# Token-major attention outputs, x turned by DMA, and v cast in GpSimd-queue DMAs

## The chip, the cores and the metric

One Trainium2 chip, one of its cores. The metric is the device time of one execution in microseconds. Each kernel ran several times; medians are given with the number of runs. A ratio is the mean time of one kernel's fast runs over that of the other's fast runs of the same rounds, with a 95% interval, so it is not quite the ratio of the two medians. Runs that the chip made in its slower state (a lower granted clock and a time some per cent longer) are left out of every ratio; the medians are over all runs, slow ones included. Profiles show one execution; its span is some 1.5 to 2 us shorter than the time.

## The reference

Two stages in a row. A gated linear attention over 4 batches of 8 heads, 768 tokens each, head size 48:

```
state[t] = sigmoid(f_logit[t]) * state[t-1] + outer(k[t], v[t])
y[t]     = q[t] @ state[t]                      # per batch and head
```

Then, with x the 3072 tokens by 384 columns that the heads' outputs make side by side:

```
h = x @ w_in                  # 384 -> 2048
out = (h * cos(h)) @ w_out    # 2048 -> 384, float32
```

Inputs and output are float32. `q`, `k`, `v` and `f_logit` lie in DRAM as (batch, head, token, 48), so what one token and one head have in a row is 48 numbers, 192 bytes.

## The kernel before

The tokens are cut into 24 chunks of 128. A chunk loads f, v, k and q (192 KB each), makes decayed q and k in bf16 (`qk`), transposes them (`qkt`: by TensorE for the first six chunks, by DMA later), multiplies them to masked scores (`am`), updates the state (`sz`), and makes the attention output. A list scheduler in the kernel's own Python (class `Plan`) places all operations before anything is emitted: it gives each a cost and a delay, and its order becomes the fixed order of instructions on each engine.

The attention output is made with features on partitions, directly as `xT`, the form that the second stage needs. Heads of 48 do not fit blocks of 128, so v and the state lie in zero-padded tiles and windows of 128 columns are cut out of them: 16 matmuls of 128 columns for a chunk with a state, from two kinds:

```python
VW = D + 128
vzS = slots("vz", 4, [128, H * VW + 128], zero=700.0)    # zero-padded v, bf16
...
P.op({"POOL": 510.0}, lambda e: nc.gpsimd.tensor_copy(   # cast of v, one per chunk
    out=vz.ap[:, 128:].rearrange(...)[:, :, 0:D], in_=vf.ap), reads=[vf], writes=[vz], prio=prio)
...
if kind == "a":                                           # 10 of these
    nc.tensor.matmul(o[:, t, :], lhsT=vz.ap[:, w0:w0 + 128],
                     rhs=ams[n // 4].ap[:, n % 4, :], **fl)
else:                                                     # 6 of these
    nc.tensor.matmul(o[:, t, :], lhsT=S_in.ap[:, n, w0:w0 + 128],
                     rhs=qdt.ap[:, n, :], **fl)
```

The loads (192-byte pieces):

```python
ap = src[b, :, c * C:(c + 1) * C, :].rearrange("h p d -> p h d")
...
P.op({"SP": 1080.0}, lambda e, t=t, ap=ap: nc.sync.dma_start(out=t.ap, in_=ap),
     writes=[t], prio=prio, lat=2200.0)
...
P.op({"SP": 2000.0}, lambda e: nc.sync.dma_start_transpose(out=qkt.ap, in_=qk.ap), ...)
```

The eight weight loads go through the GpSimd queue with a cast, and cos is a sine with a bias read from a tile (`bias=halfpi`).

Of the kernel before, what the change touches and what calls it, by code (L numbers as in the profile page):

```python
# [91 lines left out]
class Op:  # L92
    __slots__ = ("seq", "eng", "fn", "prio", "table", "deps", "vals", "alloc", "start",
                 "end", "lat", "waiting", "after", "grp", "frees")


class Plan:


    SEM = 70.0  # L100

# [3 lines left out]
    def op(self, eng, fn, reads=(), writes=(), prio=0.0, table=None, lat=0.0, grp=None):  # L105
        o = Op()
        o.seq, o.fn, o.prio, o.table, o.lat, o.grp = len(self.ops), fn, prio, table, lat, grp
        o.eng, o.frees = eng, None
        o.deps, o.alloc, o.vals = set(), [], []
        for v in reads:  # L110
            o.deps.update(v.writers)
        for v in writes:
            w = getattr(v, "whole", v)
            if w.pool is not None:
                o.alloc.append(w)
            if v.writers:

                o.deps.add(v.writers[-1])
        for v in list(reads) + list(writes):
            v = getattr(v, "whole", v)  # L120
            if v.pool is not None and v not in o.vals:
                o.vals.append(v)
                v.uses += 1
        for v in writes:
            v.writers.append(o)
        o.after = []
        self.ops.append(o)
        return o
# [6 lines left out]
    def run(self):  # L135
        engs = ("PE", "ACT", "DVE", "POOL", "SP")
        free = dict.fromkeys(engs, 0.0)
        table, lock = "E", None
        left = {}
# [9 lines left out]
        while len(order) < n:  # L149
            best = None  # L150
            for o in ready:
                at = max([d.end + (0.0 if e0 == d.eng == "PE" else self.SEM)
                          for d in o.deps for e0 in (next(iter(o.eng)),)], default=0.0)
                ok = True
                for v in o.alloc:
                    if v.slot is not None:
                        continue
                    b = v.pool.best()
                    if b is None:
                        ok = False  # L160
                        break
                    at = max(at, b[0] + self.SEM)
                if not ok:
                    continue
                pick = None
                for e, cost in o.eng.items():
                    if e == "ACT" and lock is not None and o.grp != lock and o.table is not None:
                        continue
                    s = max(at, free[e])
                    sw = 1300.0 if e == "ACT" and o.table not in (None, table) else 0.0  # L170
                    if pick is None or s + cost + sw < pick[0]:
                        pick = (s + cost + sw, s, e, cost)
                if pick is None:
                    continue
                key = (pick[1], o.prio, o.seq)
                if best is None or key < best[0]:
                    best = (key, pick[1], o, pick[2], pick[3])
# [16 lines left out]
            o.start, o.end = s, s + cost + o.lat  # L194
            free[e] = s + cost
            o.eng = e
# [20 lines left out]
def kernel(  # L217
# [10 lines left out]
    nc = tc.nc  # L228
# [12 lines left out]
    NPE = 6  # L241
# [31 lines left out]
    vS = slots("v", nld, [128, H, D], F32)  # L273
# [4 lines left out]
    VW = D + 128  # L278
    vzS = slots("vz", 4, [128, H * VW + 128], zero=700.0)
    qktS = slots("qkt", 4, [128, 3 * NP, C])  # L280
    amS = slots("am", 4, [128, 4, C])
    SW = 128 + 2 * D + 128
    szS = slots("sz", 3, [128, NP, SW], zero=650.0)
# [26 lines left out]
    def load_weights(part, i, prio):  # L310
        if part == 0:
            dst = w_in_v[i]
            src = moe_w_in.rearrange("(km p) f -> p km f", p=128)[:, :, i * 512:(i + 1) * 512]
        else:
            dst = w_out_v[i]
            src = moe_w_out.rearrange("(kf p) m -> p kf m", p=128)[:, i * 4:(i + 1) * 4, :]
        o = P.op({"SP": 2000.0}, lambda e, dst=dst, src=src: nc.gpsimd.dma_start(
            out=dst.ap, in_=src), writes=[dst], prio=prio, lat=2500.0)
        o.deps.add(first_v[0])
# [5 lines left out]
    first_v = []  # L325

    def chunk_load(b, c, prio):
        vals = []
        for pool, src in ((fS, f_logit), (vS, v), (kS, k), (qS, q)):
            t = Val(pool)  # L330
            ap = src[b, :, c * C:(c + 1) * C, :].rearrange("h p d -> p h d")
            if prio < 1 and pool in (kS, qS):
                P.op({"ACT": 600.0}, lambda e, t=t, ap=ap: nc.scalar.dma_start(out=t.ap, in_=ap),
                     writes=[t], prio=prio, lat=3300.0)
            elif prio < 2 and pool in (vS, qS):
                o = P.op({"POOL": 1000.0}, lambda e, t=t, ap=ap: nc.gpsimd.dma_start(out=t.ap, in_=ap),
                         writes=[t], prio=prio, lat=3300.0)
            else:
                P.op({"SP": 1080.0}, lambda e, t=t, ap=ap: nc.sync.dma_start(out=t.ap, in_=ap),  # L339
                     writes=[t], prio=prio, lat=2200.0)  # L340
            vals.append(t)
        return vals
# [42 lines left out]
    def attend(b, c, ld, bt, bi, prio):  # L385
# [3 lines left out]
        qk, vz = Val(qkS), Val(vzS)  # L389
# [9 lines left out]
        for par in range(2):  # L399
            P.op({"POOL": 550.0, "DVE": 350.0} if fast else {"POOL": 550.0}, lambda e, par=par: E(e).tensor_mul(  # L400
                out=ktd[par].ap, in0=kf.ap[:, par:H:2, :],
                in1=bi.ap.rearrange("p (h d) -> p h d", d=D)[:, par:H:2, :]),
                reads=[kf, bi], writes=[ktd[par]], prio=prio)
        o = P.op({"POOL": 510.0}, lambda e: nc.gpsimd.tensor_copy(  # L404
            out=vz.ap[:, 128:].rearrange("p (h w) -> p h w", w=VW)[:, :, 0:D], in_=vf.ap),
            reads=[vf], writes=[vz], prio=prio)
        first_v.append(o)
# [27 lines left out]
        else:  # L435
            P.op({"SP": 2000.0}, lambda e: nc.sync.dma_start_transpose(out=qkt.ap, in_=qk.ap),
                 reads=[qtd] + ktd, writes=[qdt] + kz, prio=prio, lat=2500.0)
# [22 lines left out]
        if c < NCH - 1:  # L460
            ps, S_out = Val(miS), Val(szS)

            def pes(e):
                o = ps.ap[:, 0:H * D].rearrange("p (h d) -> p h d", d=D)
                for h in range(H):
                    nc.tensor.matmul(o[:, h, :], lhsT=qk.ap[:, (NP + h) * C:(NP + h + 1) * C],  # L466
                                     rhs=vz.ap[:, 128 + h * VW:128 + h * VW + D],
                                     start=(h == 0), stop=(h == H - 1))
            P.op({"PE": 8 * 30.0}, pes, reads=ktd + [vz], writes=[ps], prio=prio, lat=170.0)
# [3 lines left out]
            else:  # L473
                st = Val(stS)
                P.op({"DVE": 530.0}, lambda e: nc.vector.tensor_add(  # L475
                    out=st.ap, in0=psv(), in1=S_in.ap[:, :, 128:128 + 2 * D]),
# [3 lines left out]
                out=S_out.ap[:, :, 128:128 + 2 * D], in0=srcap(),  # L480
# [5 lines left out]
        py = Val(miS)  # L486
        jobs = []
        for t in range(KM):
            for h in range(H):
                r = h * D - t * 128  # L490
                if -D < r < 128:
                    jobs.append((t, "a", h, r))
            if S_in is not None:
                for p in range(NP):
                    r = p * 2 * D - t * 128
                    if -2 * D < r < 128:
                        jobs.append((t, "s", p, r))

        def pey(e):
            o = py.ap.rearrange("p (a n) -> p a n", n=C)  # L500
            for i, (t, kind, n, r) in enumerate(jobs):
                first = all(j[0] != t for j in jobs[:i])
                fl = dict(start=(i == 0), stop=(i == len(jobs) - 1))
                if kind == "a":
                    w0 = 128 + n * VW - r
                    nc.tensor.matmul(o[:, t, :], lhsT=vz.ap[:, w0:w0 + 128],  # L506
                                     rhs=ams[n // 4].ap[:, n % 4, :], **fl)
                else:
                    w0 = 128 - r
                    nc.tensor.matmul(o[:, t, :], lhsT=S_in.ap[:, n, w0:w0 + 128],  # L510
                                     rhs=qdt.ap[:, n, :], **fl)
        rd = [vz, qdt] + ams + ([S_in] if S_in is not None else [])
        P.op({"PE": len(jobs) * N128}, pey, reads=rd, writes=[py], prio=prio, lat=170.0)
        x = xT[tok // C]

        def yev(e):
            d = x.ap
            s = py.ap[:, 0:KM * C].rearrange("p (a n) -> p a n", n=C)
            if e == "ACT":
                nc.scalar.copy(out=d, in_=s)  # L520
            else:
                nc.vector.tensor_copy(out=d, in_=s)
        P.op({"ACT": 380.0, "DVE": 530.0}, yev, reads=[py], writes=[x], prio=prio)


    def moe(t0, T):
# [6 lines left out]
        for j in range(KF // G):  # L533
            ph, co = Val(phS), Val(coS)

            def g1(e, j=j, ph=ph):
# [10 lines left out]
            P.op({"ACT": 640.0}, lambda e, ph=ph, co=co: nc.scalar.activation(  # L547
                out=co.ap, in_=ph.ap, func=AF.Sin, bias=halfpi),
# [6 lines left out]
        for i in range(T // 128):  # L555
# [12 lines left out]
            def ev(e, po=po, ot=ot):  # L568
# [7 lines left out]
                out=out[r0:r0 + 128, :], in_=ot.ap), reads=[ot], prio=pr, lat=2000.0)  # L576

    halfpi = cpool.tile([128, 1], F32, name="halfpi")
    nc.vector.memset(halfpi, HALF_PI)
# [59 lines left out]
```

## Time and profile before

| | before |
|---|---|
| time, median of 4 runs (lowest to highest) | 202.32 us (201.92 to 202.7) |
| span of the profiled run | 200.6 us |
| PE busy | 178.9 us |
| PE idle before 60 us / 60 to 160 us / after | 16.8 / 0.4 / 4.4 us |

The last row is worked out from windows: what PE was busy in a stretch, taken from the stretch's length. Two of them, with the columns as in the prediction below (stretch and length, PE, weight load, DVE, ACT, POOL, granted clock, DMA share, GB/s; the share is the packets' time added up, so it can pass 1):

```profile
20.00:30.00 10.00, 6.71 (x97) 5.97 (x95) 5.88 (x11) 5.60 (x9) 3.65 (x6) 0.88 1.27 211
60.00:160.00 100.00, 99.56 (x1081) 79.66 (x1079) 80.56 (x142) 87.22 (x151) 24.87 (x37) 1.00 1.01 205
```

```profile
PE ps L367 <- ACT sp L355: 6.3, 2, 5.3
PE ps L447 <- DMA qkt<-qk: 0.5, 1, 0.5
...
DVE am L452 <- PE ps L447: 3.2, 4, 1.9
```

From 60 to 160 us TensorE pauses 0.44 us in all, and in the whole execution it waits for a transposed `qkt` only once, for 0.5 us. L447 is the score product, L367 the first product of a chunk's decay. q1 is the queue of SP (SyncE), q0 that of GpSimd.

### The profile page before, as it was taken

The page shows a single profiled execution, that of the slowest core. Times are in us where ns is not written, and L with a number is a line of the kernel's source. Part 1 is how long each engine was busy: PE and PEld are TensorE (multiplying, and loading weights), DVE is VectorE, ACT ScalarE, POOL GpSimd, SP SyncE. Part 2 cuts the span into 40 slices and gives each one's busy share as a digit, 9 for nine tenths or more (in the row PEclk, how much of TensorE's full clock was granted, in tenths as well). Part 3 has the DMA queues.
Part 4 walks back from the last instruction along what each step waited for, and adds up shares of the span by engine and source line. Part 5 has one row for each costly group of instructions (what it writes and reads, how often), then busy time and mean ns, then how long its engine had stood idle before and what let it go on. Part 6 is the DMA issues. An engine that isn't in the chain of part 4 may idle for free.

```text
span 200.6 us, 5037 instructions
## 1 busy us (share of the span) xinstructions
PE 178.9 (89%) x1960; PEld 142.3 (71%) x1960; DVE 143.2 (71%) x248; ACT 151.6 (76%) x259; POOL 54.7 (27%) x86
## 2 busy tenths in 40 slices
PE   0359678989979999999999999999999999999992
PEld 0249566886859687778797887787787878678660
DVE  7865744775889979689689598597595998854500
ACT  4457745859999898798998799798796999727510
POOL 8775600230721130250201412711412315000000
PEclk9999978999999999999999999999999999999999
DMA  7999998998909999989999999899899954911012
GB/s 141 218 217 223 218 205 153 177 184 164 230 6 172 193 220 190 223 138 241 214 202 233 217 215 225 177 220 198 186 207 212 202 106 143 97 39 42 16 64 78
DMA packets 132328, 34.15 MB, mean 170 GB/s; under 512 B 125504, under 2 KB 132160, under 8 KB 132304
## 3 DMA queue, kind: packets, MB, share of 16 engines
q1 hardware_dynamic: 126320, 29.70, 73.8%
q0 software_dynamic: 3904, 3.74, 11.3%
q10 hardware_dynamic: 2080, 0.39, 1.1%
q8 instruction: 15, 0.25, 0.5%
q14 instruction: 9, 0.07, 0.1%
HBM read 25.17 MB, written 4.72 MB: 149 GB/s over the span
## 4 chain that ended last, share of the span: by engine, by line
PE 68%; DMA 13%; ACT 8%; issue 4%; POOL 2%; SPq 2%; DVE 2%; ACTq 0%; POOLq 0%
PE ps L561 28%; PE ps L540 26%; DMA qkt<-qk 5%; PE ps L447 5%; PE ps L506 4%; DMA w_in_bf<-in_moe_w_in_dram 4%; DMA v<-in_v_dram 4%; PE ps L510 2%; ACT b L377 2%; SPq L339 2%; PE ps L466 1%; ACT xT L520 1%; ACT qkt L430 1%; DVE qk L400 1%; ACT bi L377 1%
## 5 line engine op out<-in xcount | busy, mean ns | idle before, releaser
L540 PE MATMUL ps<-xT,w_in_bf 128*128 128x256 bf16 (+1 forms) x672 | 70.3, 259 | 4.8 <-DMA w_in_bf<-in_moe_w_in_dram 3.3
L551 DVE TENSOR_TENSOR gT<-ps,cosh 128x512 bf16<-128x512 f32 x96 | 60.7, 683 | 17.1 <-ACT cosh L547 17.0
L561 PE MATMUL ps<-w_out_bf,gT 128*128 128x384 bf16 x384 | 71.1, 329 | 0.0
L547 ACT ACTIVATE cosh<-ps,halfpi 128x512 bf16<-128x512 f32 x96 | 59.7, 694 | 10.1 <-PE ps L540 9.8
L540 PEld LDWEIGHTS <-w_in_bf 128*128 128x128 bf16 x672 | 57.5, 99 | 12.1 <-DMA w_in_bf<-in_moe_w_in_dram 3.6
L561 PEld LDWEIGHTS <-gT 128*128 128x128 bf16 x384 | 36.1, 99 | 19.9 <-issue 1.0
L452 DVE TENSOR_TENSOR am<-ps,umask 128x512 bf16<-128x512 f32 x48 | 31.0, 683 | 4.1 <-PE ps L447 3.2
L404 POOL CAST vz<-v 128x384 bf16<-128x384 f32 x24 | 12.8, 534 | 52.7 <-DMA v<-in_v_dram 44.0
L400 POOL TENSOR_TENSOR qk<-k,bi 128x192 bf16<-128x192 f32 x20 | 13.5, 679 | 38.5 <-ACT bi L377 29.4
L395 DVE TENSOR_TENSOR qk<-q,b 128x384 bf16<-128x384 f32 x21 | 12.5, 595 | 14.5 <-ACT b L377 14.5
L506 PE MATMUL ps<-am,vz 128*128 128x128 bf16 x240 | 22.3, 223 | 0.0
L570 ACT COPY ot<-ps 128x384 f32<-128x384 f32 x20 | 9.5, 475 | 13.9 <-PE ps L561 13.9
L479 POOL TENSOR_TENSOR sz<-st,b 128x384 bf16<-128x384 f32 x16 | 13.2, 824 | 24.1 <-DVE st L475 24.0
L506 PEld LDWEIGHTS <-vz 128*128 128x128 bf16 x240 | 16.8, 100 | 1.4
L400 DVE TENSOR_TENSOR qk<-k,bi 128x192 bf16<-128x192 f32 x28 | 17.4, 636 | 0.0
L606 ACT ACT_TABLE_LOAD x12 | 15.4, 1283 | 2.2 <-issue 2.0
L447 PE MATMUL ps<-qkt 128*128 128x128 bf16 x192 | 15.9, 223 | 1.3 <-ACT qkt L430 0.7
L510 PE MATMUL ps<-qkt,sz 128*128 128x128 bf16 x120 | 16.5, 219 | 0.0
L547 ACT ACT_TABLE_LOAD x12 | 15.4, 1283 | 0.2
L447 PEld LDWEIGHTS <-qkt 128*128 128x128 bf16 x192 | 12.5, 99 | 3.3 <-DMA qkt<-qk 1.6
L377 ACT ACTIVATE b<-ps 128x388 f32<-128x388 f32 x24 | 12.1, 503 | 2.9 <-PE ps L370 1.8
L367 PE MATMUL ps<-sp,umask 128*128 128x384 bf16 x24 | 8.0, 345 | 6.4 <-ACT sp L355 6.3
(38 smaller groups left out, 143.4 us busy)
## 6 DMA issues: line engine op xcount, KB each, us to landing
f<-in_f_logit_dram SPq DMA_DIRECT2D x24, 192.0 KB, 3.8
out_dram<-ot SPq DMA_DIRECT2D x24, 192.0 KB, 3.1
k<-in_k_dram SPq DMA_DIRECT2D x23, 192.0 KB, 4.1
v<-in_v_dram SPq DMA_DIRECT2D x22, 192.0 KB, 4.1
q<-in_q_dram SPq DMA_DIRECT2D x22, 192.0 KB, 4.0
w_in_bf<-in_moe_w_in_dram POOLq DMA_DIRECT2D x4, 384.0 KB, 6.1
w_out_bf<-in_moe_w_out_dram POOLq DMA_DIRECT2D x4, 384.0 KB, 8.8
v<-in_v_dram POOLq DMA_DIRECT2D x2, 192.0 KB, 6.2
```

The costliest lines, as they stand in the source:

```text
L377: nc.scalar.activation(out=o.ap, in_=pc.ap[:, 0:n], func=AF.Exp, scale=s)
L400: P.op({"POOL": 550.0, "DVE": 350.0} if fast else {"POOL": 550.0}, lambda e, par=par: E(e).tensor_mul(out=ktd[par].ap, in0=kf.ap[:, par:H: ...
L447: nc.tensor.matmul(o[:, i, :], lhsT=kz[g].ap[:, i, :], rhs=qdt.ap[:, h // 2, :], start=(i == 0), stop=(i == 3))
L452: nc.vector.tensor_mul(out=am.ap, in0=pa.ap.rearrange("p (a n) -> p a n", n=C), in1=umask[:, None, :].broadcast_to([128, 4, C]))
L479: P.op(cost, lambda e: E(e).tensor_mul(out=S_out.ap[:, :, 128:128 + 2 * D], in0=srcap(), in1=bt.ap[:, H * D:, None].broadcast_to([128, NP, ...
L506: nc.tensor.matmul(o[:, t, :], lhsT=vz.ap[:, w0:w0 + 128], rhs=ams[n // 4].ap[:, n % 4, :], **fl)
L510: nc.tensor.matmul(o[:, t, :], lhsT=S_in.ap[:, n, w0:w0 + 128], rhs=qdt.ap[:, n, :], **fl)
L540: nc.tensor.matmul(ph.ap[:, g * T:(g + 1) * T], lhsT=w_in_bf[:, m, f0:f0 + 128], rhs=x[:, m, :], start=(g == 0 and m == 0), stop=(g == G - ...
L547: P.op({"ACT": 640.0}, lambda e, ph=ph, co=co: nc.scalar.activation(out=co.ap, in_=ph.ap, func=AF.Sin, bias=halfpi), reads=[ph], writes=[c ...
L551: P.op({"DVE": 650.0}, lambda e, ph=ph, co=co, gv=gv: nc.vector.tensor_mul(out=gv.ap, in0=ph.ap.rearrange("p (g t) -> p g t", t=T), in1=co ...
L561: nc.tensor.matmul(po.ap[:, 0:d_model], lhsT=gT.ap[:, j, i * 128:(i + 1) * 128], rhs=w_out_bf[:, j, :], start=(j == 0), stop=(j == KF - 1))
L606: nc.scalar.preload_act_table_set("natural_log_exp_and_others")
```

## The change

Its intent: TensorE is the bound, so make the attention output with fewer TensorE columns. With tokens on partitions (token-major below), the masked scores are the stationary operand and v moves (8 matmuls of 48 columns), then the transposed q is stationary and the state moves (4 of 96). No padding is needed. The result `y` has to be turned to `xT`: by TensorE for the first eight chunks, by a DMA transpose on SP afterwards. v comes as bf16 through a casting DMA on the GpSimd queue, so the cast instruction goes. Weights wait for k products of given chunks instead of the first cast of v. The sine takes its bias as an immediate. The scheduler gets a model of the two DMA queues and new delays. In the code, `NPX` is the number of chunks whose x TensorE turns, `NPE` the same for `qkt`. The core of the diff, cut:

```diff
-    NPE = 6
+    GATES = [1, 2, 3, 4]
+    NPE, NPX, VAHEAD = 6, 8, 2
...
-    vS = slots("v", nld, [128, H, D], F32)
+    vS = slots("v", 8, [128, H, D])
...                                               # weights
-        o = P.op({"SP": 2000.0}, lambda e, ...: nc.gpsimd.dma_start(...), ..., lat=2500.0)
-        o.deps.add(first_v[0])
+        o = P.op({"POOL": 850.0}, lambda e, ...: nc.gpsimd.dma_start(...), ..., lat=2200.0,
+                 dma=2400.0 if part == 0 else 2200.0)
+        gate(o, 0 if part == 0 else GATES[i])
...                                               # loads
+            eng, dma = {"SP": 650.0}, nc.sync
+            if pool is vS:
+                eng, dma = {"POOL": 850.0}, nc.gpsimd
...                                               # output
+                nc.tensor.matmul(o[:, h, :], lhsT=ams[h // 4].ap[:, h % 4, :], rhs=vf.ap[:, h, :],
+                                 start=(h == 0), stop=(S_in is None and h == H - 1))
+            for p in range(NP if S_in is not None else 0):
+                nc.tensor.matmul(py.ap[:, p * 2 * D:(p + 1) * 2 * D], lhsT=qdt.ap[:, p, :],
+                                 rhs=S_in.ap[:, p, :], start=False, stop=(p == NP - 1))
...                                               # copy of y, then x
+        if tok < NPX * C:
+            ... nc.tensor.transpose(out=pxv()[:, t, :], in_=yt.ap[:, t * C:(t + 1) * C], identity=ident)
+        else:
+            P.op({"SP": 700.0}, lambda e: nc.sync.dma_start_transpose(out=x.ap, in_=yt.ap),
+                 reads=[yt], writes=[x], prio=prio, lat=2000.0, dma=480.0)
...                                               # cos
-                out=co.ap, in_=ph.ap, func=AF.Sin, bias=halfpi),
+                out=co.ap, in_=ph.ap, func=AF.Sin, bias=HALF_PI),
...                                               # scheduler
+                    if o.dma and e == "SP":
+                        s = max(s, ring[0] - self.RING)
```

## The prediction

> **What bounds the kernel now.** I read the page's busy shares and its 40 slices first, then the windows by stage, then the chain of waits in order of time, then the groups by form. The page:
>
> ```profile
> PE 178.9 (89%) x1960; PEld 142.3 (71%) x1960; DVE 143.2 (71%) x248; ACT 151.6 (76%) x259; POOL 54.7 (27%) x86
> PE   0359678989979999999999999999999999999992
> PEclk9999978999999999999999999999999999999999
> DMA  7999998998909999989999999899899954911012
> ```
>
> TensorE is the busiest engine. A slice is 5 us: PE is part empty for the first 25 to 30 us and full afterwards, so there are two stages with different limits. The windows divide them:
>
> ```profile
> 20.00:26.40 6.40, 3.13 (x58) 2.84 (x55) 3.91 (x7) 3.58 (x6) 3.65 (x6) 1.00 1.26 216
> 26.40:32.00 5.60, 5.36 (x48) 4.08 (x49) 2.95 (x5) 2.24 (x4) 0.00 (x0) 0.70 1.29 202
> 98.00:120.00 22.00, 21.94 (x245) 17.98 (x242) 17.52 (x32) 19.80 (x36) 4.83 (x7) 1.00 1.06 216
> ```
>
> After the stretch and its length the columns are PE, weight load, DVE, ACT, POOL, granted clock, DMA share, GB/s. From 98 to 120 us PE is busy 21.94 of 22: every TensorE nanosecond taken out there can shorten the kernel, unless ACT (19.80 of 22, 90%) or the DMA becomes the limit. From 26.4 to 32 the clock was only 0.70, after the pause before it. The chain of waits names that pause:
>
> ```profile
> 12.47 0.10 POOL w_in_bf L317
> 14.95 0.75 POOL w_in_bf L317
> 18.65 7.73 DMA w_in_bf<-in_moe_w_in_dram
> 26.43 2.89 PE ps L540 x36
> 84.24 0.17 PE ps L506 x3
> 84.51 0.22 PE ps L506 x4
> 84.85 0.17 PE ps L506 x3
> 181.81 5.24 PE ps L540 x48
> ```
>
> The last quarter of the first weight is issued only at 18.65 us, because weight issues stand in the GpSimd stream between casts of v, each waiting for its data; it lands at 26.4. The three L506 pieces, with the L510 pairs in the gaps, are one chunk's attention output: 84.24 to 85.17, 0.93 us for 16 matmuls. The groups by form give the changed instructions:
>
> ```profile
> L547 ACT ACTIVATE cosh<-ps,halfpi 128x512 bf16<-128x512 f32 x96 | 59.7, 694 | 10.1 <-PE ps L540 9.8
> L506 PE MATMUL ps<-am,vz 128*128 128x128 bf16 x240 | 22.3, 223 | 0.0
> L510 PE MATMUL ps<-qkt,sz 128*128 128x128 bf16 x120 | 16.5, 219 | 0.0
> L466 PE MATMUL ps<-vz,qk 128*128 128x48 bf16 x160 | 7.6, 187 | 0.2
> L404 POOL CAST vz<-v 128x384 bf16<-128x384 f32 x24 | 12.8, 534 | 52.7 <-DMA v<-in_v_dram 44.0
> ```
>
> The 223 ns of a matmul is its latency, not its price in a stream. For the price I take lengths in the chain: ten L506 take 0.56 us (56 ns each), eight 48-column L466 0.20 us (25 ns), 48 256-column L540 5.24 us (109 ns).
>
> **What the Trainium skill says.** "TensorE: Matmul & The Clock Gate", section "Back-to-back issue gap", gives N/2.4 + 2.5 ns for a warm matmul of N moving columns, with a floor near 25 ns: 56, 109 and 25 ns for N of 128, 256 and 48. The trace agrees with all three, so I use 42.5 ns for the new N of 96, an estimate from that formula. That section also warns of about 81 ns a pair at N = 128 when weights are loaded each time; this trace shows 56, and 25 for L466, which also loads weights for each matmul. "ScalarE: Activation LUTs", section "What ACT_TABLE_LOAD costs", prices a pointer bias at about 93 ns over an immediate one. The before trace has only the pointer form at this width (694 ns), so no run yet shows it. "DMA: Bandwidth & Descriptors", section "SWDGE vs HWDGE vs iDMA", says a cast in a DMA needs the GpSimd path, and under "Issuing engines are not separate DMA queues" that all paths share the same 16 engines. Moving v is therefore no extra bandwidth. The trace fits: from 20 to 26.4 us, with both queues at work, the rate is 216 GB/s, the same as in 98 to 120 with mainly one.
>
> **The change part by part.**
>
> TensorE. Removed: 240 + 120 matmuls of 128 columns at 56 ns, 20.2 us. Added: 192 of 48 columns at 25 ns, 4.8 us; 80 of 96 columns at 42.5 ns, 3.4 us; 24 transposes (x of the first eight chunks, three each) at 56 ns, 1.3 us. Net 9.5 against 20.2: 10.7 us less. Chunks 0 and 1 lie in the idle start and hold about 0.6 of it, so about 10 us falls in the full stage, where it counts. Per pair of chunks, about 13.7 us of PE before (the chain's evictions of x at 85.17 and 153.46 are five pairs apart) becomes about 12.8.
>
> The start. Weight issues no longer depend on the cast of v but on the k product of chunk 0. In the before trace bi of chunk 0 ends at 6.8 us; two GpSimd products of 0.68 us follow, and the instruction order of the changed kernel then has the four weight issues in a row, 0.8 us each: the last at about 10.6 to 11.5 us instead of 18.65. Transfers took 5.3 to 7.7 us alone and four now overlap, so I put the last landing at 19 to 22 us, not 26.4. The pauses on weights (0.7 and 2.6 us) and the slow clock behind them (5.6 us at 0.70, some 1.7 us lost) should mostly go. I count 5 us in all, since x of chunk 0 now comes later by a second copy.
>
> ScalarE. 96 sines cheaper by about 90 ns: 8.6 us. Four table loads fewer (24 to 20, 1.28 us each): 5.1 us. Copies from PSUM: y and x together go from 13 to 22, out copies 20 to 15, qkt 10 to 8: about +0.8 us. Net 13 us less, near 139. It was 90% busy in the full stage, so this keeps it off the path while PE shortens; by itself it earns nothing.
>
> VectorE. Zeroing of the padded tiles goes (about 4 us), nine k products move to GpSimd (9 x 0.64 = 5.7 us), two q products come (+1.2) and five more out copies (+2.7); about 6 us less.
>
> GpSimd. Casts go (12.8 us); 22 more v issues at about 0.99 us come (21.8 us), nine k products at 0.68 (6.1 us). About 10 us more, near 65 of 190: off the path by its share.
>
> DMA. The SP ring loses 22 v loads and gains 16 x transposes. Between 91.2 and 98.9 us it issued eight loads and an output at 0.85 us apiece; two qkt transposes hold the queue 3.7 us. An x transpose has 3 blocks to qkt's 12, so about 0.46 us. Per pair the ring goes from about 8 x 0.85 + 3.7 + 1.4 = 11.9 us to 6 x 0.85 + 3.7 + 0.9 + 1.4 = 11.1, while two cast loads of v take a share of the same engines. At the same engine cost as before, 1.7, the sum is 12.8: as long as the PE pair.
>
> Sum: 200.6 - 10 - 5 = 185.6. Against it I set 2 us of new bubbles where PE waits for an x transpose. The span becomes about 187.6; time was 1.8 us above the span, so 189.
>
> **The rivals.**
>
> First: the DMA becomes the limit. For it: 12.8 us of queue work per 12.8 us of PE, and x now makes an extra trip through a ring in which a qkt transpose took 4.8 to 4.9 us at 72.7 and 168.2. Against it: there are six f, k and q buffers and eight v buffers, loads run chunks ahead, in the before trace the DMA drops to 5 tenths and less from 160 us, and the first eight chunks take no x transpose. If it were right, PE would lose 1 us or more a pair, and the time would be 194 to 199.
>
> Second: the GpSimd stream becomes the wait. It is in order, holds the state update and now most k products, and a v issue must wait for its gate and its buffer. For it: GpSimd already fed the head in the chain (POOL pieces between 12 and 19 us). Against it: 65 of 190 us. If right, DVE and PE wait on sz or qk and the result is 192 to 196.
>
> Third: the weights come early at the cost of chunks 2 and 3. In the before trace SP issues took 4.0 to 4.5 us each while weights moved (18.6 to 32 us). Then the start earns nothing: 193 to 195.
>
> Fourth: everything is hidden behind ACT at 90%, and the time stays near 200. The cheaper sine speaks against it.
>
> **Range and chances.** The 10 us is sturdy: instruction counts times stream prices from the trace, in a stage where PE is full. The 5 us at the start is loose (0 to 8), as are the bubbles (0 to 6). So 189, with 184.5 to 195 for 8 in 10. To miss 2%, that is to stay above 198.3, the first rival would have to take nearly all: chance of faster 0.94, the same 0.05, slower 0.01.
>
> **What would show it.** Right: the new output matmuls take about 0.37 us a chunk in the chain, and PE busy falls; PE is full from about 20 us, with no clock near 0.7 at 26 to 32; the sine reads about 600 ns; ACT is near 139 us and GpSimd near 65. Wrong: PE idle put down to the DMA of xT or of qkt in mid-kernel (first rival), waits on GpSimd's sz or qk (second), first PE pauses on f, k or v after 15 us (third), or new 48-column matmuls at well over 25 ns because am weights do not load behind them.

## More of the kernel before

The DMA queues (packets, MB, and the time that the packets took as a share of 16 engines' span) and three lines of the waits (what waited, for what; us in total, times, the longest):

```profile
q1 hardware_dynamic: 126320, 29.70, 73.8%
q0 software_dynamic: 3904, 3.74, 11.3%
```

## The result, and the profile after

| | before | after |
|---|---|---|
| time, median of 4 runs | 202.32 us (201.92 to 202.7) | 209.77 us (209.25 to 211.85) |
| ratio after / before | | 1.0388, 95% 1.0315 to 1.0461: slower |
| span of the profiled run | 200.6 | 208.1 |
| PE busy | 178.9 | 174.3 |
| PE idle before 60 / 60 to 160 / after | 16.8 / 0.4 / 4.4 | 16.7 / 13.1 / 4.0 |

The kernel got 3.9% slower where 6.6% less had been predicted. The last two rows add up to the span, and so they say where the time went: PE's work fell by 4.6 us, not by 10.7, and its pauses grew by 12.1 us in all: by 12.6 us between 60 and 160 us, while the rest shrank by 0.5. The page after:

```profile
PE 174.3 (84%) x1896; PEld 135.3 (65%) x1896; DVE 138.5 (67%) x241; ACT 141.9 (68%) x257; POOL 62.7 (30%) x88
PE   0682399979999979969969789795995999999992
PEclk9998569999999999999999999999699999999998
DMA  7999999999999999999999999999999811200222
```

The row of PE has holes in mid-kernel where the kernel before had nines, and the DMA row is all nines until about 160 us, where before it dipped several times. The same two windows after:

```profile
20.00:30.00 10.00, 5.95 (x62) 5.78 (x62) 2.25 (x5) 5.73 (x10) 2.81 (x4) 0.53 1.43 163
60.00:160.00 100.00, 86.95 (x937) 65.30 (x934) 73.60 (x125) 78.76 (x143) 34.54 (x44) 0.98 1.24 194
```

In the first, PE is busy 5.95 us instead of 6.71, but does 62 matmuls instead of 97, at a granted clock of 0.53 instead of 0.88. In the second it is busy 87 of 100 us, ACT and DVE less than before too (78.8 against 87.2, and 73.6 against 80.6), while the DMA share rose and the bytes per second fell. No engine has become the bound; all of them wait. The waits say for what:

```profile
PE ps L392 <- ACT sp L380: 12.3, 2, 7.0
PE ps L471 <- DMA qkt<-qk: 7.4, 5, 2.4
PE ps L560 <- DMA xT<-y: 3.5, 3, 1.7
...
DVE am L476 <- PE ps L471: 17.6, 11, 4.7
```

L392 is the first product of a chunk's decay, L471 the score product, L560 the first product of the second stage. The waits for `qkt` went from 0.5 to 7.4 us, those for `xT` are new. DVE then waits 17.6 us (3.2 before) for score products that are themselves late. Pieces of the chain of waits, in order of time (start, us, what):

```profile
9.54 13.30 DMA f<-in_f_logit_dram
...
32.72 0.20 PE ps L515 x8
32.92 0.17 PE ps L518 x4
...
69.23 6.14 DMA qkt<-qk
...
87.67 4.91 DMA xT<-y
...
137.23 7.58 DMA qkt<-qk
153.87 6.36 DMA qkt<-qk
```

L515 and L518 are the new output matmuls: 0.37 us a chunk instead of 0.93, exactly as computed. Around them stand transfers of 5 to 13 us. A load of f issued at 9.54 us takes 13.30 us to land, and PE stands still from 17 to 24 us; before, that transfer did not appear in the chain. The pressure in this stretch is seen on the SP queue's own timeline, where the next loads, whose issues take 0.80 us in the mean from 60 to 160 us, are held for up to 5.3 us while the weights and the first loads of v move:

```profile
14.07 5.32 SPq L362 DMA_DIRECT2D q<-in_q_dram  x1
19.43 3.58 SPq L362 DMA_DIRECT2D f<-in_f_logit_dram  x1
```

The queues after:

```profile
q1 hardware_dynamic: 111136, 27.14, 69.7%
q0 software_dynamic: 28672, 5.51, 31.4%
```

v's traffic moved from q1 to q0, but the sum of the shares went from 86.8% to 102.7% of the span (all queues), for 0.8 MB less. The growth on q0, 3,904 to 28,672 packets, is the casting loads of v, and it looks like the culprit. The first experiment shows that it is not.

A last reading needs a sum. From the timeline of the SP queue between 60 and 160 us I took the mean time that one issue of each kind held the queue, and from these the queue's work for two chunks, with the number of pieces that two chunks have:

| mean us of one issue | loads | qkt | xT | out | two chunks | ratio to before |
|---|---|---|---|---|---|---|
| before | 8 x 0.80 | 2 x 1.59 | | 2 x 0.91 | 11.4 | 1 |
| after | 6 x 0.80 | 2 x 1.90 | 2 x 1.72 | 2 x 0.85 | 13.8 | 1.0388 |

Against it stand about 13.7 us of PE work for two chunks before and 12.8 after, from the prediction's working. The queue had slack before, and has none after: its work has become longer than PE's. In these 100 us SP was issuing 84.6 us before and 94.2 us after. These means may be cause and symptom at once, since an issue can be held by what is ahead of it; the experiments have to tell. For the x transpose the shortest issue helps. Duration in ns, lowest/median/highest, after:

```profile
L460 SPq DMA_TRANSPOSE qkt<-qk x18: 1278/1425/4190, 59.3 to 162.4; - x18
L542 SPq DMA_TRANSPOSE xT<-y x16: 1178/1263/3124, 84.0 to 178.2; - x16
```

`qkt` has four times the bytes of `xT` (384 KB and 96 KB by their shapes), and its shortest issue is only 0.1 us longer. In all ten profiles with x by DMA, this one and those of the experiments below, the shortest issue of `xT` took 1.18 us and the median 1.18 to 1.26: so this much looks like its own cost and not that of a crowded queue.

### The profile page after: what moved, and what is told of

It reads as the page before. It is cut to its first block, busy times and chain, and to the rows that moved or that the text cites. A ratio compares the mean times of both kernels' runs of the same rounds, so it can differ in the third digit from the quotient of the medians.

```text
span 208.1 us, 4899 instructions
## 1 busy us (share of the span) xinstructions
PE 174.3 (84%) x1896; PEld 135.3 (65%) x1896; DVE 138.5 (67%) x241; ACT 141.9 (68%) x257; POOL 62.7 (30%) x88
## 3 DMA queue, kind: packets, MB, share of 16 engines
q0 software_dynamic: 28672, 5.51, 31.4%
## 4 chain that ended last, share of the span: by engine, by line
PE 52%; DMA 25%; ACT 7%; DVE 6%; SPq 5%; issue 3%; ACTq 0%; DVEq 0%
PE ps L560 23%; PE ps L581 19%; DMA qkt<-qk 14%; DMA f<-in_f_logit_dram 6%; SPq L362 5%; DMA xT<-y 4%; PE ps L471 4%; DVE am L476 2%; DVE gT L571 2%; ACT cosh L567 2%; PE ps L515 1%; PE ps L392 1%; PE ps L445 1%; ACT L567 1%; PE ps L518 1%
## 5 line engine op out<-in xcount | busy, mean ns | idle before, releaser
L560 PE MATMUL ps<-xT,w_in_bf 128*128 128x256 bf16 (+1 forms) x672 | 70.2, 261 | 3.8 <-DMA xT<-y 3.5
L560 PEld LDWEIGHTS <-w_in_bf 128*128 128x128 bf16 x672 | 59.2, 100 | 11.2 <-DMA xT<-y 3.8
L567 ACT ACTIVATE cosh<-ps 128x512 bf16<-128x512 f32 x96 | 54.7, 600 | 11.2 <-PE ps L560 6.6
L476 DVE TENSOR_TENSOR am<-ps,umask 128x512 bf16<-128x512 f32 x48 | 30.8, 684 | 18.9 <-PE ps L471 17.6
L425 POOL TENSOR_TENSOR qk<-k,bi 128x192 bf16<-128x192 f32 x29 | 18.8, 656 | 45.2 <-ACT bi L402 26.7
L420 DVE TENSOR_TENSOR qk<-q,b 128x384 bf16<-128x384 f32 x23 | 14.5, 630 | 13.7 <-DMA q<-in_q_dram 4.5
L471 PE MATMUL ps<-qkt 128*128 128x128 bf16 x192 | 17.2, 234 | 7.5 <-DMA qkt<-qk 7.4
L362 POOL DMA_DIRECT2D v<-in_v_dram x24 | 22.4, 934 | 0.0
L471 PEld LDWEIGHTS <-qkt 128*128 128x128 bf16 x192 | 13.4, 105 | 10.5 <-DMA qkt<-qk 9.3
L590 ACT COPY ot<-ps 128x384 f32<-128x384 f32 x15 | 7.2, 481 | 17.0 <-PE ps L581 16.9
L392 PE MATMUL ps<-sp,umask 128*128 128x384 bf16 x24 | 8.5, 365 | 12.3 <-ACT sp L380 12.3
L377 ACT ACTIVATE f<-f 128x384 f32<-128x384 f32 x24 | 11.6, 517 | 8.1 <-DMA f<-in_f_logit_dram 8.0
L525 ACT CAST y<-ps 128x384 bf16<-128x384 f32 x20 | 9.7, 487 | 8.3 <-PE ps L518 6.3
L395 PEld LDWEIGHTS <-sp 128*128 128x128 bf16 x96 | 6.1, 101 | 13.1 <-issue 11.6
L623 ACT ACT_TABLE_LOAD x10 | 12.8, 1283 | 2.2 <-issue 2.0
L567 ACT ACT_TABLE_LOAD x10 | 12.8, 1283 | 0.2
L425 DVE TENSOR_TENSOR qk<-k,bi 128x192 bf16<-128x192 f32 x19 | 12.1, 645 | 0.3 <-ACT bi L402 0.3
## 6 DMA issues: line engine op xcount, KB each, us to landing
w_out_bf<-in_moe_w_out_dram POOLq DMA_DIRECT2D x4, 384.0 KB, 11.7
```

The lines of the kernel that those rows point to most:

```text
L362: o = P.op(eng, lambda e, t=t, ap=ap, dma=dma: dma.dma_start(out=t.ap, in_=ap), writes=[t], prio=prio, lat=2000.0, dma=950.0)
L420: P.op({"POOL": 1000.0, "DVE": 560.0} if fast else {"POOL": 1000.0}, lambda e: E(e).tensor_mul(out=qtd.ap, in0=qf.ap, in1=bt.ap[:, 0:H * D ...
L425: o = P.op({"POOL": 550.0, "DVE": 350.0} if fast and tok else {"POOL": 550.0}, lambda e, par=par: E(e).tensor_mul(out=ktd[par].ap, in0=kf. ...
L471: nc.tensor.matmul(o[:, i, :], lhsT=kz[g].ap[:, i, :], rhs=qdt.ap[:, h // 2, :], start=(i == 0), stop=(i == 3))
L476: nc.vector.tensor_mul(out=am.ap, in0=pa.ap.rearrange("p (a n) -> p a n", n=C), in1=umask[:, None, :].broadcast_to([128, 4, C]))
L560: nc.tensor.matmul(ph.ap[:, g * T:(g + 1) * T], lhsT=w_in_bf[:, m, f0:f0 + 128], rhs=x[:, m, :], start=(g == 0 and m == 0), stop=(g == G - ...
```

## The experiments

Eighteen kernels ran. The expectations are quoted. Five profiled runs fell in the slow state (no cast, x by TensorE, changed operations with the old plan, token-major with x by DMA, and the same with a long delay).

The ideas: (a) the casting loads of v load the DMA engines; (b) x's trip through a DMA transpose; (c) weights that come early and in a row starve the first chunks; (d) the new scheduling model, not the operations, orders things badly; (e) ScalarE, still the second busiest engine, holds the gain back; (f) loads in 192-byte pieces use up what the DMA engines can do, and the change leaves no slack for that.

### Parts of the change undone

**No cast.** v is loaded as float32 on the same queue in the same order, and the matmuls read the upper halves of the numbers in place (correct within tolerance).

```diff
-    vS = slots("v", 8, [128, H, D])
+    vS = slots("v", 8, [128, H, D], F32)
-  rhs=vf.ap[:, h, :]
+  rhs=vf.ap.bitcast(BF16)[:, h, 1::2]          # both products that read v
```

> The changed kernel with every instruction in the same place, but v is loaded as float32 on the same GpSimd queue without a cast, and the matmuls read the upper half of each word in place (a truncated v, so a slightly less exact result). Theory C (the cast makes the v loads costly for the DMA engines, which starves chunk 2 at the start and delays transposes later): the GpSimd queue's share falls from 31% to under 18%, its packets from 28672 to under 6000, and the time falls from 209.8 to 193 to 200. Theory X (the x transposes and their wait in the SP ring cost the time): 206 to 210. Theory W (the weights issued in a row starve chunk 2 at the start): 205 to 210, with the same TensorE pause from 17 to 24 us.

Measured: 208.64 us, ratio 1.0321 (1.0252 to 1.039). The packets (a count, which the state does not change) of q0 fell from 28,672 to 5,248. So idea (a) falls: four fifths of that queue's packets gone, and only about 0.7 points of the ratio with them, less than the intervals' width. (The bytes written go up, 5.51 to 7.87 MB, since v stays float32.)

**v on the SP queue, x by TensorE, and both.** The first kernel loads v as float32 with the other loads (read in place as above), the second turns x of every chunk on TensorE, the third does both.

```diff
-            if pool is vS:                                 # v on SP
-                eng, dma = {"POOL": 850.0}, nc.gpsimd
-            elif prio < 1 and pool is not fS:
+            if prio < 1 and pool is not fS:

-    NPE, NPX, VAHEAD = 6, 8, 2                              # x by TensorE
+    NPE, NPX, VAHEAD = 6, 24, 2
```

> The changed kernel with v as float32 on the SP queue, as in the kernel before, read by the matmuls in place (no cast anywhere). Theory C: 194 to 200, since the GpSimd queue holds only the weights; the SP ring is longer by 22 loads, so not better than e1 by much. Theory X: 207 to 212, as the ring in which x waits is longer. Theory W: 205 to 210.

> The changed kernel with all 24 chunks of x turned by TensorE (48 more transposes, 16 more copies out of PSUM) instead of 16 by DMA. Theory X: TensorE no longer waits for xT, 196 to 201. Theory C: the qkt transposes still land late and the start is unchanged, 204 to 209. Theory W: 205 to 210.

> Both: v as float32 on SP read in place, x always by TensorE; what remains of the change is the token-major output, the cheaper sine and the weights in a row. Theories C and X each: at most what the better of e2 and e3 gives, less 2 to 5 us: 190 to 196. Theory W: still 203 or more, with the TensorE pause at the start.

| v | x of chunks 8 to 23 | median us | ratio to before (95%) |
|---|---|---|---|
| GpSimd queue, cast | DMA (the change) | 209.77 | 1.0388 (1.0315 to 1.0461) |
| SP queue | DMA | 211.02 | 1.0452 (1.0379 to 1.0525) |
| GpSimd queue, cast | TensorE | 210.8 | 1.0361 (1.0252 to 1.0471) |
| SP queue | TensorE | 203.38 | 1.0072 (1.0009 to 1.0134) |

Each of the two costs 3 to 4 points by itself, and the second then costs nothing more. With both undone the kernel is level with the one before, not faster. That is why undoing one part alone, the obvious experiment, shows nothing: 1.0452 or 1.0361 against 1.0388. Compared with the last row, the DMA trip of x costs 3.8 points and the move of v 2.9, but both together 3.2. With v on SP the start is healthy again (PE 7.78 of 10 us busy from 20 to 30 us at a clock of 1.00, where the change had 5.95 at 0.53), and mid-kernel is worse still (85.2 of 100). In all three the list scheduler places everything anew, so the order of instructions changes with the part that is undone.

**Weights staggered.** The quarters of `w_in` wait for chunks 0, 0, 1 and 2 instead of all for chunk 0.

```diff
-        gate(o, 0 if part == 0 else GATES[i])
+        gate(o, [0, 0, 1, 2][i] if part == 0 else GATES[i])
```

> The changed kernel with the four quarters of the first weight gated on the k products of chunks 0, 0, 1, 2 instead of all on chunk 0. Theory W for the start (the weights in a row hold back f of chunk 3, whose decay stands ahead of the first layer in TensorE's order, so TensorE stands still from 17 to 24 us and then runs at half clock to about 30): the pause shrinks to under 3 us and the time falls to 203 to 206. If the start is made up for later by other waits: 208 to 211.

Measured: 212.51 us, ratio 1.0539 (1.0467 to 1.0612). The pause did not shrink, against the expectation: the longest wait is 7.1 us (7.0 in the change), and PE is busy 0.29 of the 7 us from 17 to 24. The record of the clock reads 1.00 from 20 to 30 us instead of 0.53, but the products after the pause were just as slow:

```profile
PE ps L392 <- ACT sp L380: 12.5, 2, 7.1
```

```profile
26.65 1.49 PE L560 MATMUL ps<-xT,w_in_bf 128*128 128x128 bf16 x12
27.93 0.53 PE L536 MATMUL ps<-ident,y 128*128 128x128 bf16 x3
```

From start to start, twelve products of 128 columns took 1.28 us, 107 ns each, in this kernel as in the change (26.03 to 27.31 us there), where 56 ns is the price in the full stage. So this run does not cure the start, and cannot say what the start costs; mid-kernel fell to 85.4 us of PE in 100. Staggering the weights in this way is no remedy; whether the weights are what makes the first loads late (idea c) stays open.

### Operations or schedule

The changed operations with the scheduler's old assumptions (no queue model, old delays), and the operations of before with the new ones:

```diff
-                    if o.dma and e == "SP":                 # changed kernel, old plan (cut)
-                        s = max(s, ring[0] - self.RING)
...
-                 reads=[yt], writes=[x], prio=prio, lat=2000.0, dma=480.0)
+                 reads=[yt], writes=[x], prio=prio, lat=2500.0)
```

> The changed kernel's operations (token-major output, x by DMA, cast v), ordered with the latencies that the list scheduler of the kernel before assumed (no ring model). Theory S (the new scheduler assumptions are too short, so the in-order engines wait for transfers and the waits pass from engine to engine): 194 to 201. Theory O (the operations themselves, wherever they stand, load the DMA too much): 206 to 212.

> The operations of the kernel before, ordered with the scheduler assumptions of the changed kernel (ring model, shorter latencies). Theory S: 206 to 212, TensorE idle in mid-kernel as in the changed kernel. Theory O: 199 to 204.

Measured: 217.33 us, ratio 1.0637 (1.0576 to 1.0697; profile slow), and 205.57 us, ratio 1.0193 (1.0133 to 1.0252). The new plan makes the old operations about 2% slower but the changed ones about 2.5% faster than the old plan would. So (d) is not the reason: the changed operations lose with either plan.

Now the parts put one at a time into the kernel before, with its plan. First only the token-major output, x turned by TensorE, v cast by GpSimd into a tile without padding:

```diff
+                nc.tensor.matmul(o[:, h, :], lhsT=ams[h // 4].ap[:, h % 4, :], rhs=vz.ap[:, h, :], ...)
+                nc.tensor.matmul(py.ap[:, p * 2 * D:(p + 1) * 2 * D], lhsT=qdt.ap[:, p, :], rhs=S_in.ap[:, p, :], ...)
+    NPE, NPX = 6, 24
```

> The kernel before with the token-major output alone: v cast by GpSimd into a compact tile, x turned by TensorE in all chunks, old scheduler assumptions, old sine and old weight gates. TensorE loses 20.2 us of streams and gains 8.2 plus 4.0 for 72 transposes; 24 more copies out of PSUM come on ACT or DVE (about 10 us). Theories S and O both: 194 to 199. If the token-major form itself is at fault (weight loads of the masked scores not hidden): 202 or more.

Then the same with x of chunks 8 to 23 by DMA, one number:

```diff
-    NPE, NPX = 6, 24
+    NPE, NPX = 6, 8
```

> As e7, but x of chunks 8 to 23 is turned by DMA, with the old scheduler assumptions (700 ns on SP, 2.5 us to land). Theory S with x harmless in itself: within 2 us of e7. Theory X (the x transfers cost by themselves): 4 us or more above e7, with TensorE or its weight loads waiting for xT.

Measured: 201.09 us, ratio 0.996 (0.9904 to 1.0017), and 213.72 us, ratio 1.0494 (1.0421 to 1.0567). One window of each (the second profile is of the slow state, its clock is 0.97):

```profile
60.00:160.00 100.00, 96.56 (x1070) 75.66 (x1070) 86.45 (x149) 90.95 (x156) 28.38 (x40) 1.00 1.02 202
```

```profile
60.00:160.00 100.00, 88.69 (x934) 67.86 (x932) 75.29 (x127) 80.17 (x133) 24.53 (x37) 0.97 0.96 192
```

Turning x of sixteen chunks on the SP queue instead of TensorE cost 5.3 points of the ratio, some 10.8 us. (One number is edited, but the scheduler then orders all engines anew, so this is the trip with the order that it brings.) The queue's sum for two chunks went from 11.4 to 13.6 us. This is (b), and it is the largest single effect that I found. The first of the two says something as important: the heart of the change, with nothing else, gains nothing clear, although PE is busy only 173.2 us instead of 178.9.

Was the delay of x merely too short in the plan? The scheduler was told 6 us for it:

```diff
-                 reads=[yt], writes=[x], prio=prio, lat=2500.0)
+                 reads=[yt], writes=[x], prio=prio, lat=6000.0)
```

> e8 (token-major output, x of chunks 8 to 23 by DMA, old scheduler) with the scheduler told that an x transpose lands after 6 us instead of 2.5. Theory X1 (x by DMA is only late against the order, 3 us of slack cures it): 200 to 204. Theory X2 (the x transposes load the SP ring and its in-order waits, and no order cures that): 208 to 214.

Measured: 216.07 us, ratio 1.0676 (1.0594 to 1.0759; profile slow). No: planning for a later x did not help.

**The sine.** The immediate bias added to the token-major kernel, and to the kernel before alone:

```diff
-                out=co.ap, in_=ph.ap, func=AF.Sin, bias=halfpi),
+                out=co.ap, in_=ph.ap, func=AF.Sin, bias=HALF_PI),
```

> e7 (token-major output, x by TensorE, everything else as before) plus the sine with an immediate bias, which takes about 9 us off ScalarE. Theory A (in e7 the saved TensorE time turned into waits on ScalarE and VectorE, which carry 24 more copies): 195 to 199. If TensorE were still the bound in e7, or the waits came from DMA alone: 200 to 202.

> The kernel before with only the sine's bias made immediate. Theory A's other side: TensorE is full here, so a cheaper ScalarE gains next to nothing, 200 to 202.5. If ScalarE was already a co-bound: 197 to 199.

Measured: 203.01 us, ratio 1.0065 (1.0018 to 1.0112), and 200.43 us, ratio 0.9941 (0.9889 to 0.9992). Idea (e) falls: 9 us less of ScalarE (96 x 94 ns) is worth nothing in the first and 0.6% in the second. The second has the lowest time of the correct kernels here, though its interval overlaps with that of the token-major one.

**Less DMA work in the token-major kernel.** v read in place without a cast instruction, and qkt of the first twelve chunks by TensorE instead of six:

```diff
-    NPE, NPX = 6, 24
+    NPE, NPX = 12, 24
```

> A correct candidate: e9 with v read in place as the upper half of its float32 words (no cast at all), and q and k of 12 chunks instead of 6 turned by TensorE, which takes about 11 us off the SP ring. Theory D: 195 to 199. Theory L, or if the added copies out of PSUM on ACT and DVE bind: 200 to 205.

Measured: 205.0 us, ratio 1.0162 (1.0087 to 1.0237). SP was issuing only 66 of the 100 us from 60 to 160. But the six chunks' transposes went to TensorE, whose busy time rose from 173.4 us (the kernel with the sine) to 180.1, and it was busy 97.2 of the 100 us: the run took load off the DMA by giving it to the bound engine, so it says little of what the DMA alone costs.

### The loads made cheap

The direct test of (f). Every load of f, k, q and v takes 128 contiguous rows of 1536 bytes from the same tensor instead of 192-byte pieces. The bytes, the tiles, the queues and the order on every engine are the same, as the edit is in the address that is read alone (and the page below counts the same instructions as the page after); the data are the wrong tokens, so the result is wrong.

```diff
-            ap = src[b, :, c * C:(c + 1) * C, :].rearrange("h p d -> p h d")
+            ap = src.rearrange("b h s d -> (b h s d)").rearrange(
+                "(n p h d) -> n p h d", p=C, h=H, d=D)[b * NCH + c]
```

In the changed kernel:

> The changed kernel, every instruction in the same place, but each f, k, q and v load reads 128 contiguous rows of 1536 bytes instead of 1024 pieces of 192 bytes: same bytes and tiles, wrong data on purpose. Theory D (the DMA engines' supply is the bound that the change ran into): the loads take about half the DMA time, the pauses on f, qkt and xT shrink, 186 to 194. Theory L (in-order waits and latencies, whatever the load): 204 to 210.

Measured: 192.06 us (191.88 to 194.11), ratio 0.9557 (0.9492 to 0.9621). Its page, its windows and its queues:

```profile
PE 169.3 (89%) x1896; PEld 132.3 (69%) x1896; DVE 138.2 (73%) x241; ACT 140.6 (74%) x257; POOL 54.1 (28%) x88
```

```profile
20.00:30.00 10.00, 7.03 (x109) 6.52 (x107) 5.91 (x10) 4.87 (x9) 1.50 (x3) 0.87 1.18 272
60.00:160.00 100.00, 97.76 (x1097) 76.03 (x1095) 86.91 (x148) 83.43 (x154) 31.06 (x46) 1.00 0.88 193
```

```profile
q1 hardware_dynamic: 48416, 27.14, 55.1%
q0 software_dynamic: 7168, 5.51, 20.9%
```

With the same instructions and the same megabytes, the predicted gain is there: PE's work is 9.6 us less than before (10.7 predicted), its pauses from 60 to 160 us are 2.2 us instead of 13.1, and the time lies within the predicted range. So the loss, 17.7 us between the medians 209.77 and 192.06 (of two rounds; 8.3 points of the ratios), is there only while the loads keep the DMA busy so long. What runs out is not told apart: the cheap loads shorten both the issue on SP (0.80 to 0.55 us) and the packets' time on the 16 engines (102.7% to 77.5% of the span, all queues). The queue's sum for two chunks is 6 x 0.55 + 2 x 1.87 + 2 x 1.23 + 2 x 0.54 = 10.6 us, again under PE's 12.8.

In which stage? The same edit for chunks 0 to 7 alone, then for chunks 8 to 23 alone, again in the same order:

```diff
+  ... if b * NCH + c >= 8 else <contiguous rows>      # first kernel: early loads cheap
+  ... if b * NCH + c < 8 else <contiguous rows>       # second kernel: late loads cheap
```

> The changed kernel, identical order, only chunks 0 to 7 loaded as 128 contiguous rows of 1536 bytes (wrong data on purpose); chunks 8 to 23 in pieces of 192 bytes as in the changed kernel (209.8; all 24 cheap: 192.1). If the loss is made at the start (late f and k while the weights move, third rival), most of the 17.7 us is won here: 194 to 199. If it is made in mid-kernel (first rival), little is won: 203 to 207, the pause of PE before 24 us shrinks to a few us, and PE stays at 85 to 90 us busy of 60 to 160.

> The same with only chunks 8 to 23 as contiguous rows. Mid-kernel theory: most of the gain is here, 194 to 199, PE 95 or more busy of 60 to 160, the pause before 24 us unchanged. Start theory: 203 to 207. If the two gains add up to about 17.7 the stages are independent; if each alone gains little, the lateness of either stage is enough to hold the in-order engines back.

Measured: 201.26 us, ratio 0.9924 (0.9884 to 0.9964), and 199.13 us, ratio 0.9885 (0.9845 to 0.9924). The windows of the first kernel, then of the second:

```profile
20.00:30.00 10.00, 6.57 (x100) 6.13 (x98) 4.89 (x8) 4.45 (x9) 0.98 (x3) 0.77 1.21 226
60.00:160.00 100.00, 91.69 (x992) 70.06 (x991) 79.96 (x135) 82.10 (x148) 35.43 (x45) 0.98 1.21 196
```

```profile
20.00:30.00 10.00, 5.27 (x52) 5.10 (x52) 1.97 (x4) 5.20 (x10) 2.79 (x4) 0.51 1.43 164
60.00:160.00 100.00, 97.77 (x1074) 76.69 (x1073) 84.35 (x143) 86.80 (x159) 31.49 (x46) 1.00 0.94 206
```

Neither stage alone was to blame, against what I had expected of both runs: 4.6 points of the ratio come back with the early loads and 5.0 with the late ones, against 8.3 with all, so the two gains nearly add (9.6). Early loads cheap mend the start, 100 matmuls from 20 to 30 us instead of 62 and PE busy 3.80 of the 7 us from 17 to 24 instead of 0.03; late ones leave that hole as it is and mend mid-kernel, where PE pauses 2.2 us instead of 13.1.

The same edit in the kernel before, and in the token-major kernel with the sine:

> The kernel before with the same cheap loads (wrong data on purpose). TensorE was full from 60 to 160 us, so theory D expects only the start and the few late pauses back: 195 to 199. Theory L: 200 to 202.

> e9 (token-major output, x by TensorE, cheap sine, old scheduler) with the cheap loads (wrong data on purpose). Theory D: the TensorE work saved shows at last, 188 to 194 and below e14. Theory L: 200 to 203.

Measured: 203.73 us, ratio 1.0114 (1.0067 to 1.0161), and 206.09 us, ratio 1.022 (1.017 to 1.0271). Neither gains, the second least of all. So the kernel before is not bound by its loads, and the small 192-byte pieces cost it nothing, while they cost the changed kernel 8.3 points. That the reason is the queue's work, longer than PE's only in the changed kernel, fits the sums and is argued. Why these two kernels came out slower with cheap loads was not looked into. The token-major output in the old plan is held by something else.

### The queue's sum over all runs

| two chunks on the SP queue, us | kernels (ratio to before) |
|---|---|
| 13.6 to 14.7 | the change (1.039), no cast (1.032), v on SP (1.045), old plan (1.064), token-major with x by DMA (1.049), with long delay (1.068), weights staggered (1.054) |
| 12.4 to 13.1 | x by TensorE (1.036), x by TensorE and v on SP (1.007), before with new plan (1.019) |
| 10.9 to 11.7 | before (1), token-major (0.996), with sine (1.0065), before with sine (0.994), less DMA (1.016) |
| cheap loads | 13.6, early ones (0.992); 10.8, late ones (0.989); 10.6, all (0.956); 8.3, token-major (1.022); 8.1, before (1.011) |

The sums are taken as above, each from one profile; for the five profiles in the slow state some of the length of an issue may be the state's. Every correct kernel with more than 13.5 us is slower by 3% or more, none below 12 us is slower by 2%. The kernels with cheap loads break the pattern at both ends: 13.6 us and 0.8% faster, where only the start was mended, and 8.3 us and 2.2% slower. So the sum is a correlation and not the whole of it. Two experiments make it more than that: the single-number edit that moves 11.4 to 13.6 (5.3 points lost, with a new order) and, stronger, as the order stays, the late cheap loads that move 13.8 to 10.8 (5.0 points won).

## Why the prediction was wrong

**TensorE, 10.7 us less: right.** The output takes 0.20 + 0.17 us a chunk, so 25 ns for 48 columns and 42.5 ns for 96, the two prices used. With the DMA out of the way PE's work is 9.6 us less. In the changed kernel itself the work is 5.0 us more than that (174.3 against 169.3 for the same 1,896 matmuls); the reading for which there is a number is the clock, 0.53 from 20 to 30 us against 0.87, after the pause that the loads made. (That record is no sure guide: with the weights staggered it read 1.00 over products just as slow.)

**ScalarE, 13 us less, near 139: right in kind.** The sine went from 694 to 600 ns, the total from 151.6 to 141.9, which is 9.7 us less. "By itself it earns nothing" was right too: 0.6% in the kernel before. **GpSimd near 65: right**, 62.7, and the second rival (GpSimd's stream) did not come about.

**The start, 5 us won: wrong.** The sign of the third rival came, a PE pause on f after 15 us, and it was worse than "the start earns nothing". The weights were issued early, as worked out; but a load of f among them took 13.3 us, PE stood still from 17 to 24 us, and the clock was 0.53 after it. Making only the early loads cheap gave back 4.6 points, some 9 us. That the weights are to blame for the late loads, as the rival has it, is not shown: staggering them left the pause at 7.1 us.

**The DMA: this is the step that failed.** The prediction said: "An x transpose has 3 blocks to qkt's 12, so about 0.46 us", put the SP queue (the ring) at 11.1 us and, with the v loads "at the same engine cost as before", the whole at 12.8 us, "as long as the PE pair", and then set "2 us of new bubbles" against it. Measured, an x transpose holds the queue 1.72 us, 3.7 times the estimate (1.32 in the token-major kernel, a slow profile; 1.23 with cheap loads; and in ten profiles never below 1.17, so never near 0.46), and a qkt transpose 1.90 instead of 1.85; loads were 0.80 instead of 0.85. The mis-sized term alone takes two chunks from 0.9 to 3.4 us, and the queue to 13.8. Scaling an issue by the number of blocks was the error: a quarter of the bytes lowered the shortest issue only from 1.28 to 1.18 us, and nothing in the trace of before had shown what a small transpose costs. A second slip hid the danger: the 12.8 us of the PE pair spread the 24 TensorE transposes over all chunks, but a pair whose x goes by DMA has none, and by the prediction's own prices (2 x 0.37 for 2 x 0.93) it is about 12.6 us, already less than the queue's 12.8. The term for v, in contrast, did grow in packets and packet time, and without the cast the kernel was hardly faster.

**Bubbles, 2 us: wrong by some 10 us** (12.1 us of new pauses). Two equal sums, each with its own jitter, do not make a kernel as long as one of them. On engines with a fixed order the lateness of a transfer is passed on: a late qkt holds the score product, DVE's mask behind it (17.6 us of waits instead of 3.2; with all loads cheap still 11.0, so not all of these waits cost time), and the products of other chunks that stand behind both. I had named the first rival, written that its sum was equal to PE's, and still given it next to no chance. Its ceiling, 194 to 199, left out that in a full queue the qkt transposes wait too, and that the start would lose at the same time.

**The chances** therefore rested on a wrong independence: the TensorE gain was called sturdy because the stage was full of PE, but a stage is full of one engine only as long as the next limit is not met, and that limit was 0 us away by my own sum.

**What stays open.** The token-major output in the old plan saves 5.7 us of PE's work and gains 0.4%, nothing clear; neither less ScalarE work nor cheap loads recover it, and the run with less DMA work loaded TensorE instead. Its saving reappears as pauses (96.6 us of PE in 100 instead of 99.6), with other engines waiting in turn; that the fixed order of the list is the cause is argued, not shown. Why the effects of x by DMA and of v on the GpSimd queue do not add is explained only as far as the queue's sum goes; x by TensorE with v on GpSimd has a sum of 12.4 us and is still 3.6% slower. Whether the issues on SP or the time on the DMA engines run out first, and what makes the first loads late, were not separated.

## What to carry to other kernels

When a change moves work from the bound engine to a queue, write down the queue's work per period next to the engine's, with a measured duration for every kind of transfer, and treat equality as a loss, not as a draw. A small transfer is not a small part of a large one: measure one of the very size before counting sixteen of them. And when undoing one part of a change shows nothing, undo two: a loss can have two causes, each enough alone, and each then hides the other.

## What the Trainium skill lacked or had wrong

- "Advanced Engine Details and Errata", section "X-Bar Transpose (TRN2)", says that transpose DMAs are as fast as regular ones. The page speaks of bandwidth; measured by how long an issue held the SP queue, that holds here for the large transpose and not for the small one. Before, a `qkt` of 384 KB took 1.59 us in the mean, as much as two loads of 192 KB (2 x 0.80). After, an `xT` of 96 KB took 1.72 us, and 1.18 at the least, against 0.80 for a load of twice the bytes.
- "DMA: Bandwidth & Descriptors", section "SWDGE vs HWDGE vs iDMA", names the GpSimd path as the one that casts, and does not give the price: with the cast this queue moved 28,672 packets for this kernel, without it 5,248 on the same queue. What the prediction took from it under "Issuing engines are not separate DMA queues", that this is no extra bandwidth, agrees with the trace: issues on SP were held up to 5.3 us while the GpSimd queue moved the weights.
- No page that I found says what a full queue does to engines whose order is fixed. Here 12.1 us of new PE pauses came with direct waits of PE on transposes of only 7.4 + 3.5 us, and 17.6 us of DVE's waits behind them.
